# Attention, soft mixture of experts and feed-forward layer in one kernel: scores and values taken head by head, the third scores ahead of the first values, and another order of memory and loads

## The chip, the cores and the metric

The kernel runs on one core of a Trainium2 chip. The metric is the device time of one execution in microseconds: 371.45 us is the median of three runs (371.12 to 372.02). The engines are named as in the profile: PE is TensorE's matmul, PEld its weight load, DVE is VectorE, ACT is ScalarE, POOL is GpSimd, SP is SyncE, whose queue issues all DMA transfers here.

## The reference

Three layers follow one another. The attention has 4 batches, 8 heads, 576 tokens and head size 64, with a causal window of 64 tokens. Its result, 2304 rows of 512, goes through a soft mixture of 8 experts with 4 slots each, and that through a feed-forward layer of width 2048.

```python
scores = scale * np.matmul(q, k.transpose(0, 1, 3, 2))
mask = (rel >= 0) & (rel < window)               # rel = row - column, window = 64
scores = np.where(mask, scores, -1000000000.0)
attn = np.exp(scores - scores.max(-1)) ; attn /= attn.sum(-1) + 1e-09
x = np.matmul(attn, v)                           # then laid out as [2304, 512]

logits = x @ phi                                 # phi: 512 x 32 slots
d = softmax of logits over the rows ;  c = softmax of logits over the slots
slot_input = d.T @ x                             # 32 slots x 512
h = np.maximum(slot_input[e] @ w1[e], 0.0)       # per expert e, 4 slots each
slot_out[e] = h @ w2[e]
x = c @ slot_out

h = x @ w_in
g = h * (1.0 / (1.0 + np.exp(-1.702 * h)))
out = g @ w_out
```

## The kernel before

All transfers are issued by SP in the order of the program. Each engine's instructions stand in the order in which the code is written; no scheduler reorders them. There are four stages.

**Attention, rounds 0 to 17** (the loop `for i in range(ns)`). A unit is a pair of heads of one batch: 16 units, and two rounds for the last 64 tokens. The window makes each block of 64 queries see 128 keys. Round i has the scores of unit i (`emit_s`), the transposes of the exponentials of unit i-1 (`emit_t`), the transposes of x of unit i-2 (`xt_step`), and the values of unit i-1 (`emit_pv`); ACT has the exponentials (`emit_e`, one half for each head) and the copies of the transposes, VectorE the row maxima (`nm`) and the division (`emit_norm`). In `emit_s` the mask is put in first, by four bf16 matmuls of 64x64 tiles (L315), then come 16 score matmuls on the same four tiles (L330; each leaves two records). The tile is given by the head h (rows 0-63 or 64-127 of the array) and the half j of the queries (columns):

```python
for c in range(4):
    for h in range(2):
        for j in range(2):
            ... nc.tensor.matmul(st[h][rows[j], c, :], q, k, ..., tile_position=(64 * h, 64 * j))
```

The values (L365) have the same order of loops. They read the transposed exponentials of head 0 from `ab[0]` (named pa) and those of head 1 from `ab[1]` (pl), which ACT copies one behind the other (L351). In round 1 three matmuls on the identity (L608) fill a hole.

Beside it the routing of each batch runs in the same rounds (logits, L449; exponentials; slot sums, L499), and blocks of w_in and w_out, which come as 64-bit numbers, are narrowed in pieces on ACT, POOL and VectorE (`convert`, six blocks: four of w_in, two of w_out; `N_WO` = 2).

**The tail and w1.** Behind the last round the last batch's routing is finished; the combine weights of batches 0 to 2 are turned by `c_tile` (L419: 16 matmuls of 32 columns, 32 records each). Then the w1 stage (L763): four groups of 16 matmuls.

**w2** (L804): 16 blocks of 1 MB. The first seven lie in `arena`, the memory of the attention, at multiples of 2048 words (`dslot`), and each can be fetched once the attention's pieces there are no longer read; the other nine take the slots of w1, four after each group of w1 (`load_w`, `plan`). The order is that of SP's queue: what waits there holds all behind it.

**The feed-forward stage**, 48 steps of 36 matmuls at full width: L964 and L996. The w_out blocks that were not narrowed before are fetched behind w2 and narrowed in the first steps (`out_a`, `out_b`, `out_w`, `out_c`).

Tensors of the profile: s, t, v, m are the banks of PSUM, arena and rawt hold the attention's inputs, w the weights.

Of the kernel before, what the change touches and what calls it, by code (L numbers as in the profile page):

```python
# [32 lines left out]
W_AT = {i: 1 for i in range(2, 16)}  # L33
W_AT.update({16: 1, 17: 2})
L_AT = 12


CONV_AT = {2 + 2 * n: n for n in range(6)}
# [3 lines left out]
N_WO = 2  # L42
NT = B * S
TM = 4
# [8 lines left out]
QK0 = 0  # L53
MASK0 = QK0 + 2048
IDB0 = MASK0 + 512
X0 = IDB0 + 64
V0 = X0 + 2048
XT0 = V0 + 2 * 904
X1 = XT0 + KD * MT
XL0 = X1 + 2048  # L60
LTT0 = XL0 + 1024
XLT0 = LTT0 + 256
LT0 = XLT0 + 1024
D0 = LT0 + 128
DT0 = D0 + TM * NS
PHI0 = DT0 + 2 * NS
VL0 = PHI0 + 512
QL0 = XL0 + 512
ARENA = 7 * 2048
N_E = 16  # L70
LS0 = NE * 260

# [3 lines left out]
def attention_softmoe_ffn(  # L76
# [146 lines left out]
    lt = mem(LT0, 128)  # L223
# [34 lines left out]
    load_qk(0)  # L258
    load_v(0)
    load_qk(1)  # L260
# [44 lines left out]
    def emit_s(i):  # L305
        u, t = work[i]
        st = [bank("m" if i == 1 and h else "s", (128, 4, 128)) for h in range(2)]
        rows = [slice(64 * h, 64 * h + 64) for h in range(2)]
        for h in range(2):
            for j in range(2):  # L310
                o = st[h][rows[j]]
                m = mask[rows[h], j]
                if t is not None:
                    m = mask[rows[h], 0, 1:2].to_broadcast([64, 4, 128])
                nc.tensor.matmul(  # L315
                    o, identb[rows[h], rows[h]], m,
                    start=True, stop=False, tile_position=(64 * h, 64 * j))
        for c in range(4):
            for h in range(2):
                for j in range(2):  # L320
                    r = rows[h]
                    if t is None:
                        b = qbuf(u)[r]
                        q = b[:, 64 * (2 * c + j):64 * (2 * c + j) + 64]
                        o = c - 1 if c and not j else c
                        k = two(b, 512 + 64 * c, 768 + 64 * o)
                    else:
                        b = qbuf(NU + 2 * t + j)[r, 192 * c:192 * c + 192]
                        q, k = b[:, 0:64], b[:, 64:192]
# [23 lines left out]
    def emit_pv(i):  # L353
        u, t = work[i]
        pvt[i] = [bank("v", (128, 4, 65)) for _ in range(2)]
        for c in range(4):
            for h in range(2):
# [59 lines left out]
    def c_tile(p, l):  # L417
        for j in range(4):
            nc.tensor.matmul(  # L419
                p[32 * j:32 * j + 32], l, ident, start=True, stop=True, tile_position=(0, 32 * j))  # L420

# [15 lines left out]
    def routing(b):  # L437
# [33 lines left out]

        d = mem(D0, TM * NS).rearrange("p (t s) -> p t s", t=TM)

# [73 lines left out]
        def side(t0, a, tag):  # L547
            n = min(TM, nt - t0)

            def c_turn():  # L550
                st[t0] = pq = bank(tag)[:, 0:128 * n]
                for t in range(n):
                    p = pq[:, 128 * t:128 * t + 128]
                    if b < B - 1:
                        c_tile(p, l[:, t0 + t, :])
                    else:
                        nc.tensor.transpose(
                            p, st["c", t0][:, t].rearrange("p j s -> p (j s)"), ident)
# [3 lines left out]

            return [c_turn, lambda: c_high(a, st[t0]), lambda: c_low(a, st[t0])]
# [22 lines left out]
    load_qk(2)  # L586
    nc.sync.dma_start(out=phis, in_=phi.rearrange("p (k s) -> p k s", k=KD))
    raws = [wslot() for _ in range(3)]
    ns = len(work)
    def convert(i, first):  # L590
# [13 lines left out]
    for i in range(ns):  # L604
        emit_s(i)
        if i == 1:
            for _ in range(3):
                nc.tensor.matmul(bank("v")[:, 0:128], ident, ident, start=True, stop=True)  # L608
# [8 lines left out]
        for f in early.get(i, ()):  # L617
            f()
        if i:
# [14 lines left out]
        if 0 < i < NU - 1:  # L634
# [6 lines left out]
        elif i >= NU:  # L641
            for n in range(2):
                set_ones(NU + 2 * (i - NU) + n)
        if i == L_AT:
# [6 lines left out]
        if i < 3:  # L651
            for n in range(2 * i, 2 * i + 2):
                early_load(n)
        convert(i, False)
        load_w(W_AT.get(i, 0))
# [3 lines left out]
    load_w(1)  # L659
    emit_t(ns - 1)  # L660
    xt_step(ns - 2)()
# [8 lines left out]
    load_w(2)  # L670
# [18 lines left out]

    tail_logits(0)  # L690
# [7 lines left out]
    tail_logits(1)  # L698
    m = sp.tile([128, 1], F32, tag="mrun", name="mrun")
# [10 lines left out]
    dt = mem(DT0, 2 * NS).rearrange("p (t s) -> p t s", t=2)  # L710
# [11 lines left out]
    load_w(2)  # L722
# [60 lines left out]
    for f in sides[1][2:] + sides[2][2:] + norm:  # L783
        f()
# [196 lines left out]
    def emit_o(n, between):  # L981
# [28 lines left out]
        for t in range(nt):  # L1010
# [15 lines left out]
            for q in between.pop(t, ()):  # L1026
# [3 lines left out]
    ahead = {10: [lambda: out_w(0)], 11: [lambda: out_c(0), lambda: out_w(1)],  # L1030
             12: [lambda: out_c(1)]}
# [25 lines left out]
    out_a(2)  # L1057
# [3 lines left out]
    out_b(2)  # L1061
# [9 lines left out]
    out_w(2)  # L1071
    out_c(2)
    out_a(3)
    out_b(3, (0, 1))
# [4 lines left out]
    for p, (at, bt, ms) in enumerate((  # L1079
# [8 lines left out]
    for n in range(len(steps)):  # L1088
# [7 lines left out]
        if n in todo:  # L1096
            out_b(todo[n])
        between = {}
# [11 lines left out]
        emit_o(n, between)  # L1110
        if n == 0:
            out_b(3, (2, 3))
        if n in todo or n == 1:
            low = todo.get(n, 3)
            out_w(low)
# [62 lines left out]
```

## Time and profile before

| | |
|---|---|
| median of three runs | 371.45 us |
| the profiled execution: its time | 372.59 us |
| its span, first to last instruction | 370.6 us |
| granted TensorE clock over the span | 1.00 (2.4 GHz) |
| TensorE busy | 355.0 us |
| attention, round 2's scores to the last logits | 13 to 91 us |
| w1 starts | 107.24 us |
| last w2 matmul done | 140.94 us |

A row of the timeline has the start in us from the span's start, the length in us, the engine, the line, the operation, what is written and read, the shapes, and how many instructions were merged (x32); in brackets, if there is any, the idle time of the engine before it and what ended it. Matmuls are pipelined: the starts are measured, the lengths modelled, so the work is read from start to start. PE counts the matmul records; an fp32 matmul leaves two, a transpose one.

### The profile page before, as it was taken

What the parts mean: (1) busy time and instruction counts of PE and PEld (TensorE: products, weight loads), DVE (VectorE), ACT (ScalarE), POOL (GpSimd) and SP (SyncE); (2) the same over time, 40 slices, a digit from 0 to 9 for tenths busy, and PEclk for the clock granted to TensorE, in tenths of its full rate; (3) what the DMA queues carried; (4) which work ended last, traced back from release to release, by engine and by line L of the source; (5) the groups of instructions that cost most, each with busy time, mean ns of one, the idle gap of its engine ahead of it and who ended that gap; (6) DMA issues with size and microseconds to landing.
All of it is one profiled execution on the core that took longest, in us unless ns stands there. A gap on an engine that the chain in (4) does not pass through costs nothing.

```text
span 370.6 us, 7867 instructions
## 1 busy us (share of the span) xinstructions
PE 355.0 (96%) x3091; PEld 271.5 (73%) x3091; DVE 237.8 (64%) x518; ACT 195.6 (53%) x498; POOL 47.4 (13%) x92
## 2 busy tenths in 40 slices
PE   6999999999789998999999999999999999999995
PEld 5887777768543325888778887788887888888884
DVE  3566788877356404949485969697968786262624
ACT  3798878879223205765666644555545453333330
POOL 4545666441100000000000000000000000000000
PEclk9999999999999999999999999999999999999999
DMA  7999999999999995314031314131300000031404
GB/s 268 334 404 408 412 413 409 406 381 375 398 385 370 424 392 218 107 57 135 38 113 58 113 57 130 42 113 59 113 0 2 0 0 2 0 136 37 165 6 170
DMA packets 18804, 70.87 MB, mean 191 GB/s; under 512 B 2000, under 2 KB 3408, under 8 KB 14800
## 3 DMA queue, kind: packets, MB, share of 16 engines
q1 hardware_dynamic: 18768, 70.38, 50.1%
q8 instruction: 24, 0.39, 0.4%
q14 instruction: 12, 0.10, 0.1%
HBM read 65.65 MB, written 4.72 MB: 190 GB/s over the span
## 4 chain that ended last, share of the span: by engine, by line
PE 75%; DMA 9%; ACT 8%; DVE 4%; issue 2%; SPq 0%; POOL 0%; DVEq 0%; ACTq 0%; POOLq 0%
PE s L996 18%; PE t L996 17%; PE v L996 17%; DMA w<-in_w_dram 8%; PE m L964 5%; PE v L365 3%; ACT pa L342 3%; PE s L330 3%; PE m L350 2%; DMA arena<-in_qk_dram 2%; ACT pl L351 2%; ACT pa L351 1%; PE m L499 1%; PE m L449 1%; PE s L763 1%
## 5 line engine op out<-in xcount | busy, mean ns | idle before, releaser
L952 ACT ACTIVATE r<-m 128x384 fp32r<-128x384 f32 (+1 forms) x97 | 47.5, 493 | 85.0 <-PE m L964 84.9
L977 DVE TENSOR_TENSOR r<-g,r 128x384 fp32r<-128x384 f32 x96 | 51.4, 554 | 51.3 <-ACT g L952 43.0
L996 PE MATMUL t<-w,r 128*128 128x512 f32 x288 | 75.8, 395 | 0.0
L996 PE MATMUL s<-w,r 128*128 128x512 f32 x288 | 74.3, 392 | 0.0
L996 PE MATMUL v<-w,r 128*128 128x512 f32 (+1 forms) x291 | 73.4, 387 | 0.0
L996 PEld LDWEIGHTS t<-w,r 128*128 128x128 f32 x288 | 53.8, 188 | 14.7 <-issue 4.0
L996 PEld LDWEIGHTS v<-w,r 128*128 128x128 f32 x291 | 54.3, 188 | 11.4
L996 PEld LDWEIGHTS s<-w,r 128*128 128x128 f32 x288 | 52.6, 188 | 8.5
L952 ACT ACTIVATE g<-m 128x384 f32<-128x384 f32 x96 | 47.9, 501 | 0.0
L342 ACT ACTIVATE pa<-s,nm 128x128 f32<-128x128 f32 x140 | 40.7, 399 | 6.2 <-DVE nm L335 5.7
L964 PE MATMUL m<-cT,w 128*128 128x384 f32 (+2 forms) x113 | 25.7, 319 | 0.0
L335 DVE TENSOR_REDUCE nm<-s 128x4 f32<-128x512 f32 x35 | 22.5, 684 | 4.3 <-PE s L330 3.0
L964 PEld LDWEIGHTS m<-cT,w 128*128 128x128 f32 x113 | 20.8, 188 | 4.7 <-DVE w L901 0.6
L350 PE MATMUL m<-ident,pa 128*128 128x128 f32 x144 | 19.6, 279 | 0.0
L351 ACT COPY pa<-m 128x512 f32<-128x512 f32 x18 | 10.5, 586 | 13.7 <-PE m L350 13.6
L350 PEld LDWEIGHTS m<-ident,pa 128*128 128x128 f32 x144 | 15.5, 141 | 3.0 <-issue 2.4
L330 PE MATMUL s<-arena 64*64 64x128 f32 x352 | 13.7, 271 | 2.2 <-POOL rawt L247 1.6
L763 PE MATMUL s<-w,phis 128*32 128x512 f32 x128 | 14.6, 595 | 0.5 <-DVE phis L744 0.5
L384 DVE TENSOR_TENSOR arena<-v,rs 128x256 f32<-128x256 f32 x36 | 13.6, 420 | 0.6
L330 PEld LDWEIGHTS s<-arena 64*64 64x64 f32 x352 | 11.4, 133 | 3.5 <-POOL rawt L247 2.0
L365 PE MATMUL v<-arena,pa 128*64 128x65 f32 x184 | 13.2, 227 | 0.3 <-issue 0.3
L1016 DVE TENSOR_TENSOR w<-s,w 128x512 f32<-128x512 f32 x18 | 11.6, 684 | 2.8 <-PE s L996 2.8
(206 smaller groups left out, 472.7 us busy)
## 6 DMA issues: line engine op xcount, KB each, us to landing
w<-in_w_dram SPq DMA_DIRECT2D x24, 1024.0 KB, 10.4
w<-in_w_out_dram SPq DMA_DIRECT2D x16, 512.0 KB, 3.4
arena<-in_w_dram SPq DMA_DIRECT2D x7, 1024.0 KB, 8.5
iraw<-in_w_in_dram SPq DMA_DIRECT2D x12, 512.0 KB, 3.3
arena<-in_qk_dram SPq DMA_DIRECT2D x10, 512.0 KB, 8.7
out_dram<-w SPq DMA_DIRECT2D x16, 256.0 KB, 2.1
arena<-in_vt_dram SPq DMA_DIRECT2D x13, 258.5 KB, 7.5
rawt<-in_qk_dram SPq DMA_DIRECT2D x6, 512.0 KB, 9.9
```

Source lines behind the costliest of these rows:

```text
L330: nc.tensor.matmul(st[h][rows[j], c, :], q, k, start=False, stop=(c == 3), tile_position=(64 * h, 64 * j))
L335: nc.vector.tensor_reduce(out=nm[:, h], in_=st[h], axis=AX.X, op=ALU.max, negate=True)
L342: nc.scalar.activation(out=pb[h][:, c, :], in_=st[h][:, c, :], func=ACTF.Exp, bias=nm[:, h, c:c + 1], scale=1.0)
L350: nc.tensor.transpose(tt[:, c, :], pb[h][:, c, :], ident)
L351: nc.scalar.copy(ab[h], tt)
L365: nc.tensor.matmul(pvt[i][h][64 * j:64 * j + 64, c, :], ab[h][:, c, 64 * j:64 * j + 64], v, start=True, stop=True, tile_position=(0, 64 * j))
L384: nc.vector.tensor_tensor(out=o, in0=pv[h][:, :, 1 - h:65 - h], in1=rs[:, h].unsqueeze(2).to_broadcast([128, 4, 64]), op=ALU.mult)
L763: nc.tensor.matmul(ph[32 * j:32 * j + 32, :], siT[:, kk, :], w1t[4 * r + j][:, kk, :], start=(kk == 0), stop=(kk == KD - 1), tile_position ...
L952: nc.scalar.activation(out=(gh, g)[part][:, a:e], in_=ph[:, a:e], func=ACTF.Gelu_apprx_sigmoid)
L964: nc.tensor.matmul(ph[:, c - a:e - a], mst[:, f * 128:f * 128 + 128], cT(c, e - c), start=True, stop=True)
L977: nc.vector.tensor_tensor(out=gl, in0=g, in1=gh.bitcast(F32), op=ALU.subtract)
L996: nc.tensor.matmul(accs[t][:, h], a[:, c], b[:, h], start=(first and k == 0), stop=(last and k == 2 and h.stop == 512))
```

## The change

1. In `emit_s` and `emit_pv` the loop over heads becomes the outer one: head 0's masks and eight score matmuls, then head 1's; head 0's eight value matmuls, then head 1's.
2. Round 2's scores stand in round 1, ahead of the first values; their scaling is done on VectorE. The second block of q and k is fetched ahead of the first of v; the three filling matmuls go.
3. The combine weights of batches 0 to 2 are widened four times by a copy on VectorE (`c_wide`, into rawt) and turned by whole transposes, as those of batch 3 were.
4. The arena is laid out anew, so that its seven blocks come free in another order; small pieces (D0, LT0, DT0) move to rawt. The w1 and w2 loads are issued at other rounds.
5. Raw blocks of w_in are issued earlier, two at the start, and only one block of w_out comes that early (`N_WO` = 1); the second is fetched behind w2 and narrowed in the last stage's first steps, where the third and fourth follow a step later.

```diff
-W_AT = {i: 1 for i in range(2, 16)}
-W_AT.update({16: 1, 17: 2})
+W_AT = {**{i: 1 for i in range(2, 17)}, 10:0, 15:2, 16: 2, 17: 3}
+LATE = 99
-CONV_AT = {2 + 2 * n: n for n in range(6)}
+CONV_AT = {i: n for n, i in enumerate((3, 5, 7, 9, 11))}
-N_WO = 2
+N_WO = 1
...
+X0, QK0, XT0, V0, X1, XLT0, XL0 = [2048 * n for n in range(7)]
...
+D0, LT0, DT0 = LS0 - 152, LS0 + 288, LS0 + 416
...
     load_qk(0)
+    load_qk(1)
     load_v(0)
-    load_qk(1)
+    load_qk(2)
     load_v(1)
...
                 nc.tensor.matmul(
                     o, identb[rows[h], rows[h]], m,
                     start=True, stop=False, tile_position=(64 * h, 64 * j))
-        for c in range(4):
-            for h in range(2):
+            for c in range(4):
                 for j in range(2):
...
     def emit_pv(i):
...
-        for c in range(4):
-            for h in range(2):
+        for h in range(2):
+            for c in range(4):
                 for j in range(2):
...
             def c_turn():
                 st[t0] = pq = bank(tag)[:, 0:128 * n]
                 for t in range(n):
-                    p = pq[:, 128 * t:128 * t + 128]
-                    if b < B - 1:
-                        c_tile(p, l[:, t0 + t, :])
-                    else:
-                        nc.tensor.transpose(
-                            p, st["c", t0][:, t].rearrange("p j s -> p (j s)"), ident)
+                    nc.tensor.transpose(
+                        pq[:, 128 * t:128 * t + 128],
+                        st["c", t0][:, t].rearrange("p j s -> p (j s)"), ident)
...
+            def c_wide():
+                c = rawt[:, 512 * b:512 * b + 512].rearrange(
+                    "p (t j s) -> p t j s", t=TM, j=4)
+                nc.vector.tensor_copy(c, l.unsqueeze(2).to_broadcast([128, TM, 4, NS]))
+                st["c", 0] = c
...
-    load_qk(2)
...
+    for n in range(2):
+        early_load(n)
...
     for i in range(ns):
-        emit_s(i)
-        if i == 1:
-            for _ in range(3):
-                nc.tensor.matmul(bank("v")[:, 0:128], ident, ident, start=True, stop=True)
+        if i != 2:
+            emit_s(i)
         if i:
             emit_t(i - 1)
...
+        if i == 1:
+            scale_q(2, nc.vector)
+            emit_s(2)
         if i:
             emit_pv(i - 1)
...
-        if i < 3:
-            for n in range(2 * i, 2 * i + 2):
+        if i < 2:
+            for n in range(2 * i + 2, min(2 * i + 4, FP + N_WO)):
                 early_load(n)
...
-    out_a(2)
+    out_a(1)
...
-    out_w(2)
-    out_c(2)
-    out_a(3)
-    out_b(3, (0, 1))
+    out_w(1)
+    out_c(1)
+    out_a(2)
+    out_b(2, (0, 1))
...
-            ((2, 4, 5, 6), (8, 9, 10, 12), (8, 9)),
+            ((3, 4, 5, 6), (8, 9, 10, 12), (8, 9)),
...
+        if n == 1:
+            out_b(3, (0, 1))
...
+        if n < 2:
+            out_b(n + 2, (2, 3))
+        if n in todo or n < 2:
+            low = todo.get(n, n + 2)
+            out_w(low)
         if n == 0:
-            out_b(3, (2, 3))
...
+            out_a(3)
```

The order on TensorE in round 3, from the last of its mask matmuls to the first values, before (s is the bank of the scores, pa and pl are the heads' transposed exponentials):

```order
L315 LDWEIGHTS arena
L315 MATMUL s<-arena 64x512
L330 MATMUL s<-rawt 64x128 x16
L350 MATMUL m<-ident,pa 128x128 x8
L403 MATMUL m<-ident,arena 128x128 x4
L365 MATMUL v<-arena,pa 64x65 x2
L365 MATMUL v<-arena,pl 64x65 x2
```

The same round on TensorE after, from the last mask of head 0 on (L308 are the masks, L322 the scores, L357 the values):

```order
L308 MATMUL s<-arena 64x512
L322 MATMUL s<-rawt 64x128 x8
L308 LDWEIGHTS arena
L308 MATMUL s<-arena 64x512
L308 LDWEIGHTS arena
L308 MATMUL s<-arena 64x512
L322 MATMUL s<-rawt 64x128 x8
L342 MATMUL m<-ident,pa 128x128 x8
L395 MATMUL m<-ident,arena 128x128 x4
L357 MATMUL v<-arena,pa 64x65 x8
L357 MATMUL v<-arena,pl 64x65 x8
```

The sixteen scores in one piece became twice eight with head 1's masks between them, and the values, which went from head to head in pairs, became eight and eight.

TensorE behind the last round, before (L449 are logits, L419 the turn of batch 0's combine weights, lg):

```order
L449 MATMUL m<-arena,phis 32x128 x16
L350 MATMUL m<-ident,pa 128x128 x8
L403 MATMUL m<-ident,arena 128x128 x4
L419 MATMUL s<-ident,lg_84 32x128 x16
L365 MATMUL v<-arena,pa 64x65
```

and after, where rawt holds the widened weights and L540 turns them:

```order
L436 MATMUL m<-arena,phis 32x128 x16
L342 MATMUL m<-ident,pa 128x128 x8
L395 MATMUL m<-ident,arena 128x128 x4
L540 MATMUL s<-ident,rawt 128x128 x4
L357 MATMUL v<-arena,pa 64x65
```

Sixteen matmuls of 32 columns became four transposes; they stand at the same place, ahead of the last values.

The first transfers in SP's queue before (qk and vt are the units' inputs, w takes the raw blocks of w_in):

```order
L229 DMA rawt<-in_qk_dram 128x1024
L243 DMA rawt<-in_vt_dram 128x517
L229 DMA arena<-in_qk_dram 128x1024
L243 DMA arena<-in_vt_dram 128x517
L229 DMA arena<-in_qk_dram 128x1024
L587 DMA phis<-in_phi_dram 128x128
L229 DMA rawt<-in_qk_dram 128x1024
L243 DMA arena<-in_vt_dram 128x517
L154 DMA w<-in_w_in_dram 128x1024 x2
```

and after:

```order
L221 DMA rawt<-in_qk_dram 128x1024
L221 DMA arena<-in_qk_dram 128x1024
L235 DMA rawt<-in_vt_dram 128x517
L221 DMA arena<-in_qk_dram 128x1024
L235 DMA arena<-in_vt_dram 128x517
L578 DMA phis<-in_phi_dram 128x128
L146 DMA w<-in_w_in_dram 128x1024 x2
L221 DMA rawt<-in_qk_dram 128x1024
L235 DMA arena<-in_vt_dram 128x517
```

The second qk went ahead of the first vt, and the first two raw blocks ahead of the fourth qk.

## Rows read from the trace of the kernel before

**Rows 1.** The page: busy shares, and GB/s in 40 slices of 9.27 us.

```profile
PE 355.0 (96%) x3091; PEld 271.5 (73%) x3091; DVE 237.8 (64%) x518; ACT 195.6 (53%) x498; POOL 47.4 (13%) x92
...
GB/s 268 334 404 408 412 413 409 406 381 375 398 385 370 424 392 218 107 57 135 38 113 58 113 57 130 42 113 59 113 0 2 0 0 2 0 136 37 165 6 170
```

**Rows 2.** Windows: length, busy PE, PEld, DVE, ACT, POOL; clock, DMA, GB/s.

```profile
13.00:91.00 78.00, 74.65 (x1437) 59.46 (x1434) 60.22 (x172) 64.45 (x198) 38.34 (x66) 1.00 1.01 395
107.00:141.00 34.00, 32.48 (x290) 10.57 (x290) 11.47 (x25) 6.12 (x11) 0.00 (x0) 1.00 1.00 395
```

**Rows 3.** Timeline of TensorE, a plain round: start, length, line, tiles, records.

```profile
21.19 0.48 PE L315 MATMUL s<-arena 64*64 64x512 bf16 x4
21.43 1.11 PE L330 MATMUL s<-arena 64*64 64x128 f32 x32
22.47 1.09 PE L350 MATMUL m<-ident,pa 128*128 128x128 f32 x8
23.40 0.60 PE L403 MATMUL m<-ident,arena 128*128 128x128 f32 x4
23.93 0.34 PE L365 MATMUL v<-rawt,pa 128*64 128x65 f32 x4
24.34 0.34 PE L365 MATMUL v<-rawt,pl 128*64 128x65 f32 x4
...
25.31 0.47 PE L315 MATMUL s<-arena 64*64 64x512 bf16 x4
```

**Rows 4.** Timeline of TensorE's weight loads, same round; idle before in brackets.

```profile
22.47 0.85 PEld L350 LDWEIGHTS m<-ident,pa 128*128 128x128 f32 x8 [0.17 <-issue]
```

**Rows 5.** Timeline of ACT, the same round.

```profile
23.22 0.59 ACT L351 COPY pa<-m 128x512 f32<-128x512 f32 x1 [0.49 <-PE m L350]
23.70 0.59 ACT L351 COPY pl<-m 128x512 f32<-128x512 f32 x1
```

**Rows 6.** Timeline of TensorE, values that wait for nothing, and the next masks.

```profile
39.60 0.34 PE L365 MATMUL v<-rawt,pa 128*64 128x65 f32 x4
...
40.68 0.41 PE L315 MATMUL s<-arena 64*64 64x512 bf16 x4
```

**Rows 7.** Waits: who for whom, us in total, times, longest.

```profile
PEld v L365 <- ACT pl L351: 3.0, 14, 0.2
```

**Rows 8.** Timeline of TensorE, start-up.

```profile
8.38 0.33 PE L330 MATMUL s<-arena 64*64 64x128 f32 x2 [1.61 <-POOL rawt L247]
...
9.41 1.03 PE L608 MATMUL v<-ident 128*128 128x128 f32 x6
10.28 1.04 PE L350 MATMUL m<-ident,pa 128*128 128x128 f32 x8
...
14.23 0.44 PE L350 MATMUL m<-ident,pa 128*128 128x128 f32 x2
```

**Rows 9.** Timeline of TensorE, behind the last round.

```profile
92.80 0.63 PE L419 MATMUL s<-ident,lg 128*32 128x128 f32 x12
94.72 0.85 PE L419 MATMUL s<-ident,lg 128*32 128x128 f32 x20 [1.30 <-issue]
...
107.24 1.07 PE L763 MATMUL s<-w,phis 128*32 128x512 f32 x8 [0.47 <-DVE phis L744]
```

**Rows 10.** Groups by form: a copy that widens; busy, mean ns, idle before.

```profile
L631 DVE COPY arena<-phis 128x512 f32<-128x512 f32 x1 | 0.4, 418 | 0.0
```

**Rows 11.** Timeline of TensorE, the w2 stage and its end.

```profile
126.88 4.50 PE L804 MATMUL v<-arena,rawt 128*32 128x512 f32 x40
131.19 7.35 PE L804 MATMUL v<-w,rawt 128*32 128x512 f32 x64
...
140.94 0.71 PE L755 MATMUL s<-ident 128*128 128x128 f32 x4
```

**Rows 12.** Timeline of SP's queue, the last ten issues of w2.

```profile
110.86 12.76 SPq L149 DMA_DIRECT2D w<-in_w_dram  x10
```

**Rows 13.** Window of the last stage's second step, columns as in rows 2.

```profile
151.00:155.50 4.50, 4.50 (x21) 3.79 (x22) 4.40 (x9) 2.80 (x6) 0.00 (x0) 1.00 0.37 115
```

More of the change, by code (lines that the diff above doesn't have):

```diff
@@ L50 @@
 GREATEST = float(np.uint32(0x47EFFFFF).view(np.float32))
[L53 to L60, printed above, removed]
-LTT0 = XL0 + 1024
[L62 to L68, printed above, removed]
+X0, QK0, XT0, V0, X1, XLT0, XL0 = [2048 * n for n in range(7)]
+IDB0 = V0 + 2 * 904
+PHI0 = XLT0 + KD * 256
+MASK0 = PHI0 + KD * 128
+QL0 = XL0 + 512
+LTT0 = XL0 + 1024
+VL0 = LTT0 + 256
 ARENA = 7 * 2048
@@ L222, in attention_softmoe_ffn @@
     xlT = mem(XLT0, KD * 256).rearrange("p (k n) -> p k n", k=KD)
-    lt = mem(LT0, 128)
+    lt = rawt[:, LT0:LT0 + 128]
     ltt = mem(LTT0, 256)
@@ L415, in xt_step @@
         return evac
[L417 to L420, printed above, removed]
     def c_high(a, p):
@@ L470, in dexp @@
             st["s"] = s
-        d = mem(D0, TM * NS).rearrange("p (t s) -> p t s", t=TM)
+        d = rawt[:, D0:D0 + TM * NS].rearrange("p (t s) -> p t s", t=TM)
         def turn(*ks):
@@ L561, in c_turn @@
                         [128, 128 * n], F32R, tag="ct" if t0 else "pl", name="cT")
+            def c_wide():
[3 more added lines that the diff above has]
+                st["c", 0] = c
+            if b < B - 1:
+                return [c_turn, lambda: c_high(a, st[t0]), lambda: c_low(a, st[t0]), c_wide]
             return [c_turn, lambda: c_high(a, st[t0]), lambda: c_low(a, st[t0])]
@@ L633, in attention_softmoe_ffn @@
                 phis.unsqueeze(2).to_broadcast([128, KD, 4, NS]))
-        if 0 < i < NU - 1:
+        if 1 < i < NU - 1:
             scale_q(i + 1, nc.gpsimd)
@@ L643, in attention_softmoe_ffn @@
                 set_ones(NU + 2 * (i - NU) + n)
+        if LATE <= i < ns - 1:
+            load_w(W_AT.get(i, 0))
         if i == L_AT:
@@ L650, in attention_softmoe_ffn @@
             load_v(i + 2 + (i + 2 >= NU))
-        if i < 3:
-            for n in range(2 * i, 2 * i + 2):
+        if i < 2:
+            for n in range(2 * i + 2, min(2 * i + 4, FP + N_WO)):
                 early_load(n)
         convert(i, False)
-        load_w(W_AT.get(i, 0))
+        if i < LATE or i == ns - 1:
+            load_w(W_AT.get(i, 0))
     rings.update(s=[0, 1], t=[2, 7], v=rings["v"])
     cts[0] = s1.tile([128, 1536], F32R, tag="pa", name="cT")
-    load_w(1)
+    sides[0][3]()
     emit_t(ns - 1)
+    sides[1][3]()
     xt_step(ns - 2)()
@@ L669, in attention_softmoe_ffn @@
     total()
-    load_w(2)
+    load_w(1)
     sides[0][1]()
@@ L688, in tail_logits @@
         nc.vector.tensor_reduce(out=mm[:, t:t + 1], in_=lpt[:, c], axis=AX.X, op=ALU.max)
+    sides[2][3]()
     tail_logits(0)
@@ L698, in attention_softmoe_ffn @@
     tail_logits(1)
+    load_w(1)
     m = sp.tile([128, 1], F32, tag="mrun", name="mrun")
@@ L709, in attention_softmoe_ffn @@
     gather()
-    dt = mem(DT0, 2 * NS).rearrange("p (t s) -> p t s", t=2)
+    dt = rawt[:, DT0:DT0 + 2 * NS].rearrange("p (t s) -> p t s", t=2)
     pd = bank("m", (128, 2, NS))
@@ L721, in attention_softmoe_ffn @@
                 start=True, stop=True, tile_position=(0, 32 * g))
-    load_w(2)
+    load_w(1)
     sr = sp.tile([128, 1], F32, tag="srun", name="srun")
@@ L782, in attention_softmoe_ffn @@
     turn(1)
-    for f in sides[1][2:] + sides[2][2:] + norm:
+    for f in sides[1][2:3] + sides[2][2:3] + norm:
         f()
@@ L1027, in emit_o @@
                 q()
-    ahead = {10: [lambda: out_w(0)], 11: [lambda: out_c(0), lambda: out_w(1)],
-             12: [lambda: out_c(1)]}
+    ahead = {10: [lambda: out_w(0)], 11: [lambda: out_c(0)]}
     wb = bank("s")
@@ L1060, in attention_softmoe_ffn @@
     m0[1]()
-    out_b(2)
+    out_b(1)
     emit_m1(1, "v")
@@ L1110, in attention_softmoe_ffn @@
         emit_o(n, between)
+        if n < 2:
[3 more added lines that the diff above has]
+            out_w(low)
         if n == 0:
-            out_b(3, (2, 3))
-        if n in todo or n == 1:
-            low = todo.get(n, 3)
-            out_w(low)
+            out_a(3)
         if n + 1 in more:
```

## The prediction, made before the changed kernel was run

> **What bounds the kernel now.** I read the page's busy shares and bandwidth by slice first, then the chain of waits, then TensorE's timeline of one round of the attention, and last the stretches behind it. TensorE is busy for 355.0 of 370.6 us, and from slice 2 to slice 15 the DMA engines move 334 to 424 GB/s, so two resources are full for the first 140 us [rows 1]. The reader is to see which of them a shorter or longer piece of work would move, stage by stage.
>
> In the attention, 13 to 91 us, TensorE is busy 74.65 of 78 us, at the granted clock 1.00 (2.4 GHz), and the DMA carries 395 GB/s [rows 2]. One round without routing runs from the mask matmuls at 21.19 to the next ones at 25.31: 4.12 us [rows 3]. In it the matmuls stand end to end: masks, scores, transposes of the round before, transposes of x, values. The row of the values shows the only hole: head 0's first pair starts at 23.93, head 1's at 24.34, since ACT copies head 0's transposes (pa) at 23.22 and head 1's (pl) only at 23.70 for 0.59 us [rows 3, 5]. So TensorE sets a round's length, and the wait for pl is inside it.
>
> Behind the attention the w1 stage starts at 107.24 [rows 9] and needs nothing of the DMA. The w2 stage does: five blocks pass in 126.88 to 131.19, 0.86 us each, so the 14 blocks from 126.88 on would be through at 138.95; they are through at 140.94, which is 2.0 us of waiting for the last blocks to land [rows 11]. From there to the end of the span (229.7 us) TensorE is full again. Both limits meet at 141 us: whatever TensorE gains before it is capped by the DMA unless that gains too, but whatever TensorE loses counts, less 2.0 us.
>
> **The change part by part.**
>
> Scores head by head. The 16 score matmuls of a round are 64x64 tiles; each leaves two records of 128 columns. Today the order is block, head, half, so that consecutive matmuls lie on four different tiles: 32 records between 21.43 and 22.47, less the 0.17 in which the engine goes over to the transposes (its weight load stands idle so long [rows 4]), 0.87 us or 27 ns each, which is 108 ns on each of four tiles [rows 3]. The values are two tiles wide: 32 records of 65 columns between 39.60 and 40.68, less as much again, 0.91 or 28 ns each, 57 ns on each of two tiles [rows 6]. That is 1.19 and 1.14 columns per ns and tile: a tile has its own pace, whether two or four are at work. With head 0's eight matmuls ahead of head 1's, only two tiles are at work at a time if TensorE keeps its order: 32/2 x 108 ns = 1.73 us, 0.86 more than now. The masks, four at once in 0.24 us (21.19 to 21.43), become two and two: some 0.2 more, of which 0.1 lies beside the last scores of head 0. Sum: +0.95 us a round. Nothing else in a round is idle that could take it up.
>
> The trace of before has no place where a matmul for a free tile stands behind one for a busy tile, so the cost has two ends: 0, if TensorE lets head 1 pass, and 1.1, if the second masks hide nothing. A gain is excluded, since no engine waits for the first head's scores alone: ACT comes to its exponentials only behind the pl copy. The nearest row is the values': head 0's second pair has its operand since 23.8 and still starts only behind head 1's first pair, which waited until 24.34 [rows 3, 5]. TensorE does not pass a matmul that is held. I take 0.95.
>
> The Trainium skill (TensorE: Matmul & The Clock Gate, Part 3: Packing small matmuls — row/col tiling) says that matmuls start and end in program order, and only weight loads are pulled ahead. By that the two heads cannot overlap, and the sum is the one below; were matmuls pulled ahead as weight loads are, the first rival would hold. The values' row agrees with the rule for a matmul that waits for a semaphore; for one that waits for a tile no row shows it.
>
> Values head by head. All of head 0's values then run before pl is needed. Values with the wait take 25.31 - 23.93 = 1.38 us up to the next masks, those without 40.68 - 39.60 = 1.08 [rows 3, 6]; the wait occurs 14 times [rows 7], the first at the start-up's values. So 13 x 0.30 = -3.9 us. Head 0's half takes about 0.47, to 24.4, and pl is there at 24.29. Ends: -3.9, and 0 if ACT's copy comes later.
>
> Third scores ahead of the first values. Today the second scores start at 8.38 after a wait for POOL's scaling of the second block, then come three filling matmuls (9.41 to 10.28) and the transposes; the next transposes start at 14.23 [rows 8]. Afterwards the second block is fetched one transfer earlier (258.5 KB, about 0.8 us at the 334 GB/s of slice 2 [rows 1]): scores from 7.6, 1.95 us long, no filling matmuls, transposes at 9.7, third scores (0.2 + 2.0), first values (0.2 + 0.93), next transposes at about 14.2. I count 0, between -1.0 and +1.0, and from here on the extra applies to the scores of rounds 3 to 17: 15 x 0.95 = +14.25 us.
>
> The turn of the combine weights. The first three row blocks are no longer turned by 32 small-tile records each, but widened on VectorE and transposed whole. Block 0's turn stands on the path: 92.80 to 95.57 with a stall of 1.30 in the middle [rows 9]. Four whole transposes cost 4 x 0.116 (eight took 22.47 to 23.40 [rows 3]) = 0.46, but wait for VectorE, which first has the maximum of the last logits; the widening is one copy of 128x512, 0.42 [rows 10]. I take -0.9; the ends are -1.7 (the stall goes too) and +0.2. The turns of blocks 1 and 2 lie in holes of the tail that VectorE and ACT set; 0.
>
> Arena, order of loads, w_out. w_out's second block (0.52 MB, 1.3 us at 400 GB/s) goes behind w2, the raw blocks come earlier, and the arena's regions come free in the order in which w2 takes them. All of it helps the DMA, which then is not the limit: w1 starts 9.4 us later, so the nine w2 blocks that go into w1's slots are issued from 110.9 + 9.4 = 120.3 on [rows 12], 9.44 MB at 395 GB/s end at 144.2, and TensorE wants the last at 138.95 + 9.4 = 148.4. So the 2.0 us of waiting go, and the rest of the DMA's gain buys nothing. Cover of the converted block: its VectorE work (about 1.5 us) moves into the second step of the last stage, where VectorE was busy 4.40 of 4.50 us [rows 13]; its products come a step ahead of their use, so 0, at most +0.6.
>
> Sum: +14.25 - 3.9 - 0.9 - 2.0 = +7.45 us, on the profiled execution: span 370.6 to 378.05, its time 372.59 to 380.0. The runs shown have their median at 371.45, 1.14 below that execution, so 371.45 + 7.45 = **378.9 us**.
>
> **The rivals.**
>
> 1. The two heads overlap all the same, since TensorE queues ahead and tiles are independent. For it: four tiles do run side by side. Against it: the held pair in the values. Then TensorE comes to w1 3.9 + 0.9 = 4.8 earlier, and the DMA is the limit: its last w2 block lands 1.3 earlier for w_out, and up to 0.9 earlier for the slow first two slices (268 and 334 GB/s [rows 1]). 371.45 - 1.7 = 369.8, faster. It decides as soon as a round's scores take under 1.2 us.
>
> 2. They overlap in part, say half: 15 x 0.45 = 6.75, less 3.9, 0.9 and 2.0, is 0: 371.4, the same.
>
> 3. The wait for pl stays: ACT was busy 64.45 of 78 us in the attention [rows 2], and if its copies come as late after the transposes as head 0's values are short, nothing of the 3.9 is saved: 382.8. Against it: pl was there 0.1 before it would be needed, and longer rounds give ACT time.
>
> That the change leaves TensorE's order as it was is excluded by the order above.
>
> **How the numbers follow.** Forecast 0.65, rival 1 0.20, rival 2 0.07, rival 3 0.08. A measurement of this kernel tells 0.3%, 1.1 us, from no change. Slower 0.65 + 0.08 = 0.73; the same 0.07; faster 0.20. The likeliest case alone: with 0.86 to 1.05 a round (+-1.4), the start-up (+-1.0) and the tail (+1.1, -0.8) 375.8 to 382. For 8 in 10 the range goes up to 383, which takes in rival 3, and down to 369.6, which takes in rival 2 and half of rival 1.
>
> **What would show it.** Right: the scores' 32 records with the second masks take 2.0 us up to the transposes, in two bursts; a plain round lasts 4.75 to 4.8; no wait of the values for pl; w1 starts at 116 to 117; no wait of the w2 matmuls for the DMA; the last stage still 229 to 230 us; granted clock 1.00 throughout. Wrong: scores still near 1.0 us, w1 before 104 and the w2 stage ended by a transfer (rival 1); or pl waits still 13 times (rival 3); or the last stage longer by over 1 us, which nothing here foresees.

## The result, and the profile after

The changed kernel takes 374.68 us (median of 20 runs, 372.33 to 379.12), the kernel before 370.99 beside it (20 runs); the ratio is 1.0085, 95% interval 1.006 to 1.0109: slower by about 3.2 us, where +7.45 was forecast. Two of the changed kernel's 20 runs, over 1.5% above its fastest, are left out of the ratio; of those that are left its profiled execution is one of the faster, while before's was one of the slower, so the profiles say where time went and the ratios how much. The profiled execution took 373.05 us with a span of 371.1, only 0.5 more than before's: this pair of profiles holds 0.5 of the 3.2 us. Below, 1% is 3.7 us.

The page of the changed kernel, to be held against [rows 1]; PEclk is the granted clock in tenths:

```profile
PE 359.3 (97%) x3001; PEld 278.6 (75%) x3001; DVE 241.5 (65%) x523; ACT 195.2 (53%) x498; POOL 44.9 (12%) x90
...
PEclk9999999999989999999999999999999999999999
...
GB/s 275 410 412 409 390 380 239 397 345 386 422 425 349 427 391 273 109 115 123 48 113 58 113 58 123 48 111 61 113 2 0 0 0 2 0 133 39 163 9 170
```

TensorE is 4.3 us busier, the second slice moves 410 GB/s for 334, and one slice (102 to 111 us) has a lower clock. The windows of [rows 2] now, in the same columns:

```profile
13.00:91.00 78.00, 76.87 (x1370) 64.87 (x1370) 56.69 (x162) 61.59 (x189) 37.31 (x67) 1.00 0.97 371
107.00:141.00 34.00, 33.52 (x295) 11.48 (x294) 11.07 (x24) 5.60 (x10) 0.00 (x0) 0.95 0.98 395
```

In the attention TensorE is busy for 98.6% of the time, the DMA carries less than before. TensorE's timeline of a plain round, the counterpart of [rows 3]:

```profile
20.40 0.40 PE L308 MATMUL s<-arena 64*64 64x512 bf16 x2
20.64 0.71 PE L322 MATMUL s<-arena 64*64 64x128 f32 x10
21.09 0.40 PE L308 MATMUL s<-arena 64*64 64x512 bf16 x2
21.18 1.18 PE L322 MATMUL s<-arena 64*64 64x128 f32 x22
22.30 1.09 PE L342 MATMUL m<-ident,pa 128*128 128x128 f32 x8
23.22 0.60 PE L395 MATMUL m<-ident,arena 128*128 128x128 f32 x4
23.75 0.69 PE L357 MATMUL v<-rawt,pa 128*64 128x65 f32 x16
24.27 0.64 PE L357 MATMUL v<-rawt,pl 128*64 128x65 f32 x16
24.84 0.40 PE L308 MATMUL s<-arena 64*64 64x512 bf16 x2
```

Head 0's half of the scores is 16 records, but head 1's masks start at 21.09 behind only ten of them; the other six stand behind the masks. So head 1 passes six records, three on each of two tiles (a pair, below, is one record on each of a head's two tiles). From the first mask to the transposes it is 1.90 us for 1.28, +0.62 and not +0.95. The values stand without a hole (0.93 us from first to last start, no wait for pl). The round is 4.44 us for 4.12, where 4.77 was forecast. Rounds 3 to 17 together, from the third round's masks to the last logits, are 75.15 us (15.96 to 91.11) for 73.00 (17.07 to 90.07): +2.15 and not 15 x 0.62, since most rounds of before were longer than their matmuls need (values to values, six of the nine rounds without routing took 4.12 to 4.63 us, three 3.75).

Behind the rounds, against [rows 9]:

```profile
94.35 0.66 PE L540 MATMUL s<-ident,rawt 128*128 128x128 f32 x4 [0.40 <-DVE rawt L550]
...
100.99 0.60 PE L540 MATMUL t<-ident,rawt 128*128 128x128 f32 x4
102.38 0.31 PE L714 MATMUL m<-ident,arena 32*128 32x32 f32 x2 [0.78 <-ACT arena L706]
...
103.81 0.63 PE L540 MATMUL v<-ident,rawt 128*128 128x128 f32 x4
106.53 1.05 PE L743 MATMUL m<-i4s,acc 128*128 128x32 f32 x8 [2.08 <-DVE acc L741]
108.05 5.01 PE L764 MATMUL s<-w,phis 128*32 128x512 f32 x32 [0.48 <-DVE phis L745]
```

The stall of 1.30 is gone (not by the turn, as a_ctile shows) and the turn's matmuls are short, but TensorE now waits: 0.40 for VectorE's widening copy, 0.78 for ACT, and 2.08 for VectorE ahead of psi. VectorE's and GpSimd's timelines say why:

```profile
104.44 1.93 DVE L734 TENSOR_SCALAR i4s<-i,rsl 128x32 f32<-128x32 f32 x1
104.60 2.24 DVE L741 TENSOR_TENSOR acc<-m,acc 64x256 f32<-64x256 f32 x2
```

```profile
104.51 1.83 POOL L749 MEMSET rawt<- 128x2080 f32 x1 [11.95 <-PE v L540]
```

i4s, 32 columns, takes 1.93 us and ends as GpSimd's clearing of ht does. The clearing has to wait for the last turn, which now reads its widened block out of the same tile, so it falls on i4s. The windows of TensorE (length, busy, granted clock, DMA, GB/s) show what followed the waits:

```profile
102.00:107.40 5.40, 2.63 (x24) 1.00 1.02 428
107.50:110.80 3.30, 2.82 (x17) 0.50 1.02 425
111.00:125.00 14.00, 14.00 (x127) 1.00 0.93 377
```

TensorE was busy for 2.63 of 5.40 us, and then its granted clock was 0.50 (1.2 GHz): the first w1 group took 5.01 us. w1 starts 0.8 us later than before and w2 2.2 later (126.62 for 124.44), yet w2 now waits for no transfer; its end, against [rows 11]:

```profile
133.38 7.91 PE L805 MATMUL v<-w,rawt 128*32 128x512 f32 x80
141.22 0.71 PE L756 MATMUL s<-ident 128*128 128x128 f32 x4
```

From 141.22 on to the end of the span it is 229.9 us, for 229.7.

### The profile page after: what moved, and what is told of

It is laid out like the page before. It is cut to its first block, busy times and chain, and to the rows that moved or that the text cites. A ratio compares the mean times of both kernels' runs of the same rounds, so it can differ in the third digit from the quotient of the medians.

```text
span 371.1 us, 7689 instructions
## 1 busy us (share of the span) xinstructions
PE 359.3 (97%) x3001; PEld 278.6 (75%) x3001; DVE 241.5 (65%) x523; ACT 195.2 (53%) x498; POOL 44.9 (12%) x90
## 4 chain that ended last, share of the span: by engine, by line
PE 89%; DVE 5%; ACT 3%; issue 1%; DMA 1%; DVEq 0%; ACTq 0%
PE s L997 18%; PE t L997 17%; PE v L997 17%; PE s L322 6%; PE m L965 5%; PE s L764 4%; PE v L357 4%; PE v L805 4%; PE m L342 4%; PE s L308 2%; PE m L395 2%; ACT pa L334 2%; PE m L486 1%; DMA rawt<-in_qk_dram 1%; DVE nm L327 1%
## 5 line engine op out<-in xcount | busy, mean ns | idle before, releaser
L322 PE MATMUL s<-arena 64*64 64x128 f32 x352 | 20.1, 269 | 0.1
L322 PEld LDWEIGHTS s<-arena 64*64 64x64 f32 x352 | 18.6, 133 | 1.2 <-DVE arena L231 0.4
L764 PE MATMUL s<-w,phis 128*32 128x512 f32 x128 | 15.9, 642 | 0.5 <-DVE phis L745 0.5
L933 ACT CAST w<-wf 128x512 fp32r<-128x512 f32 x15 | 9.3, 623 | 9.2 <-DVE wf L171 9.2
L308 PE MATMUL s<-arena 64*64 64x512 bf16 x70 | 14.1, 400 | 0.1
```

The lines of the kernel that those rows point to most:

```text
L308: nc.tensor.matmul(o, identb[rows[h], rows[h]], m, start=True, stop=False, tile_position=(64 * h, 64 * j))
L322: nc.tensor.matmul(st[h][rows[j], c, :], q, k, start=False, stop=(c == 3), tile_position=(64 * h, 64 * j))
L764: nc.tensor.matmul(ph[32 * j:32 * j + 32, :], siT[:, kk, :], w1t[4 * r + j][:, kk, :], start=(kk == 0), stop=(kk == KD - 1), tile_position ...
```

## The experiments

All ratios are to the kernel before run beside each, with 95% intervals. The theories: A, the loss is the collision of MEMSET and i4s with the low clock behind it; B, it is the longer scores; C, it is the low clock behind the rounds; D is on how far a matmul may pass a held one.

| kernel | scores | values | turn | other | ratio (interval) | median us |
|---|---|---|---|---|---|---|
| changed | by head | by head | widened | | 1.0085 (1.006-1.0109) | 374.68 |
| a_memset | by head | by head | widened | MEMSET later | 1.0073 (1.0047-1.0099) | 373.34 |
| a_inter | interleaved | by head | widened | | 1.0002 (0.9981-1.0023) | 370.45 |
| a_both | interleaved | by head | widened | MEMSET later | 0.9964 (0.9942-0.9987) | 369.16 |
| b_heads | by head | by head | as before | rest as before | 1.0147 (1.0116-1.0179) | 375.36 |
| b_pv | interleaved | by head | as before | rest as before | 0.9989 (0.9971-1.0007) | 370.3 |
| a_ctile | by head | by head | as before | | 1.0059 (1.0028-1.0089) | 373.05 |
| a_best | interleaved | by head | as before | | 0.9929 (0.9907-0.995) | 367.78 |
| a_rest | interleaved | interleaved | as before | | 0.9957 (0.9934-0.9979) | 368.45 |
| a_warm | by head | by head | widened | 39 idle matmuls | 1.015 (1.0106-1.0193) | 376.91 |
| a_fill | by head | by head | widened | 18 idle matmuls | 1.0062 (1.0033-1.0091) | 373.2 |
| a_both_warm | interleaved | by head | widened | MEMSET later, 27 | 0.9964 (0.9939-0.9988) | 369.53 |

**a_inter: scores interleaved again.**

```
-            for c in range(4):
+        for c in range(4):
+            for h in range(2):
                 for j in range(2):
```

> The changed kernel with the scores of the two heads interleaved again (both heads' masks first), values still head by head. Theory B (longer score rounds): a plain round falls from 4.44 to about 3.82 us (4.12 less 0.30), the last logits start 0.6 x 15 = 9 us earlier if TensorE's issue stalls stay away (tied to what the DMA queues move), some 4.5 us earlier if they come back (tied to the order of the scores); median 370 to 366, with the collision at i4s still there. Theory A (the loss is behind the rounds): the rounds are shorter but the end is set by w2's weights or the collision; median 373 to 375.

Measured: 0.83% or 3.1 us under the changed kernel, so the scores are the greater part of the loss. But the last logits come only 4 us earlier (87.15 for 91.11), not 9. Some rounds fell to 3.75 us, plain ones stayed at 4.13, and TensorE waited 2.3 us for ACT ahead of the logits: theory B with a smaller size.

**b_heads: only the two loops turned, in the kernel before.**

```
-        for c in range(4):
-            for h in range(2):
+            for c in range(4):
                 for j in range(2):
...
-        for c in range(4):
-            for h in range(2):
+        for h in range(2):
+            for c in range(4):
                 for j in range(2):
```

> The kernel before with only the two loops turned: scores and values head by head; loads, arena and order of the rounds as before. Theory B: a plain round 4.12 + 0.61 - 0.30 = 4.43 us, the last logits 0.31 x 15 = 4.7 us later, less up to 4.4 if the issue stalls go with the order of the scores; median 371.5 to 375.7, no stretch at 0.50. Theory A: no collision here, i4s stays at 0.24 us and the end follows the rounds by little: 371 to 372.

Measured: +1.47%, 5.4 us, in the range of theory B. In its trace the last logits start 6.2 us later than before's (96.28 for 90.07) and the w2 stage, which no longer waits for a transfer, ends 2.7 later (143.61 for 140.94). The rest of the change, then, gains: 0.6% between this and the changed kernel.

**b_pv: only the values turned (the second half of that diff), in the kernel before.**

> The kernel before with only the values head by head. By the prediction's step (13 waits of 0.30 us for pl go, nothing is late next): -3.9 us, ratio 0.9895. If ScalarE is next (TensorE then waits for its x copy ahead of the logits, and head 1's mask for its last exponentials, as the kernel with interleaved scores showed): 1 to 2 us, ratio 0.995 to 0.997.

Measured: -0.4 us, less than either expectation, and its interval holds zero. Its timelines show where the wait went, TensorE first, then ACT:

```profile
20.22 0.69 PE L365 MATMUL v<-arena,pa 128*64 128x65 f32 x16
20.73 0.64 PE L365 MATMUL v<-arena,pl 128*64 128x65 f32 x16
21.30 0.78 PE L315 MATMUL s<-arena 64*64 64x512 bf16 x4
21.78 1.17 PE L330 MATMUL s<-arena 64*64 64x128 f32 x32
22.88 1.09 PE L350 MATMUL m<-ident,pa 128*128 128x128 f32 x8
...
24.34 0.75 PE L365 MATMUL v<-rawt,pa 128*64 128x65 f32 x15
```

```profile
20.47 1.16 ACT L342 ACTIVATE pa<-s,nm 128x128 f32<-128x128 f32 x4
21.48 0.62 ACT L407 COPY arena<-m 128x512 f32<-128x512 f32 x1
21.94 1.20 ACT L342 ACTIVATE pa<-s,nm 128x128 f32<-128x128 f32 x4
23.63 0.59 ACT L351 COPY pa<-m 128x512 f32<-128x512 f32 x1 [0.49 <-PE m L350]
24.11 0.59 ACT L351 COPY pl<-m 128x512 f32<-128x512 f32 x1
24.59 1.16 ACT L342 ACTIVATE pa<-s,nm 128x128 f32<-128x128 f32 x4
```

The values stand end to end, as forecast, but from the masks to the transposes it is now 1.58 us for 1.28 of [rows 3]. The scores go round three banks, two a round, so head 1's pair of masks writes the bank of head 0 of the round before, which ACT's exponentials of that head still read; these begin at 20.47 behind the pl copy and end at 21.63, and the pair is held until 21.68. The round stays 4.12 us (20.22 to 24.34, values to values). So such a round of 4.12 us was a loop through two engines: exponentials of head 0 on ACT, head 1's masks and the scores of the next round on TensorE, the transposes behind them, ACT's copies pa and pl, exponentials of head 0 again. The wait for pl was slack inside it, and taking it away moved 0.30 us to the mask.

**a_mask1: both heads' masks first, scores by head.** (One run, 374.0 us.)

```
+        for h in range(2):
             for c in range(4):
                 for j in range(2):
```

The added loop makes the scores' one its own, behind the four masks.

> The changed kernel with both heads' masks ahead of both heads' scores, which stay head by head. Theory D (a matmul on a free half passes a few queued ones of a busy half, three pairs here): from the first mask to the transposes about 1.65 us in a plain round (masks 0.24, five pairs of head 0, three pairs of both together, five of head 1), against 1.89 in the changed kernel. A queue that passes nothing: 2.15 or more. One that passes freely: 1.28 as with interleaved heads.

Measured, TensorE in a round whose masks wait for nothing:

```profile
16.23 0.41 PE L308 MATMUL s<-arena 64*64 64x512 bf16 x4
16.47 1.54 PE L323 MATMUL s<-rawt 64*64 64x128 f32 x32
17.94 0.33 PE L343 MATMUL m<-ident,pa 128*128 128x128 f32 x1
```

1.71 us for 1.65 expected, far from 2.15 and from 1.28, as theory D said; it is one run, and the sizes were taken from the changed kernel. In plain rounds, where head 1's masks wait for ACT, it is 2.00 and the round 4.54, longer than the changed kernel's 4.44. Head 1's masks behind head 0's scores hide that wait, which is why the longer scores cost a plain round only 0.32.

**a_memset: the clearing held back behind siT.**

```
+    nc.gpsimd.tensor_tensor(
+        out=ht[:, 0:32], in0=siT[:, 0], in1=siT[:, 0], op=ALU.subtract)
     nc.gpsimd.memset(ht[:, 0:LS0], 0.0)
```

> The changed kernel, with GpSimd's clearing of ht (128x2080) held back by a 128x32 operation on GpSimd that reads siT, so that it starts behind VectorE's i4s and siT. Theory A (what the change loses is the collision of this MEMSET with VectorE's i4s, 1.93 us for 0.24, and the clock of 0.50 that follows TensorE's wait of 2.08): i4s back under 0.4 us, TensorE's wait ahead of psi under 0.6, no stretch at 0.50, w1 starts about 1.7 us earlier and its first group takes 3.6 for 5.0: median 3 us under the changed kernel's 374.7, about 371.6. Theory B (the loss is the longer score rounds, and DMA or something else sets w2's end): the wait goes, but w2 ends where it did; median 374 to 375.

Measured: in the profile all that theory A said (i4s 0.24 us, the wait 0.70, no stretch at 0.50, w1 at 106.94), in the time 0.12% less, within the intervals. In nine of the twelve executions the mean clock was 0.991 to 0.995, as in the changed kernel, so a low clock of that size came back in most of them, though no trace shows where. Theory A alone falls. With the scores interleaved (**a_both**, this edit and a_inter's) it gave 0.38%, 1.4 us: 369.16, near the 370 of its second case. Its profile has the low clock and no collision.

> The changed kernel with both edits: scores interleaved again and the MEMSET behind siT. Both theories added: 374.7 - 3.1 - (4.5 to 9) = 363 to 367 if nothing else ends last; if w2's weights (DMA) set the end of w2 as they did in part before (2.0 us of waits there), the gain stops at about 4 us: 370.

**a_warm: idle matmuls in the waits, too many** (one of five places shown).

```
     psi = bank("m", (128, KD, 32))
+    for _ in range(17):
+        nc.tensor.matmul(psi.rearrange("p k s -> p (k s)"), ident, ident, start=True, stop=True)
...
```

> The changed kernel with idle matmuls of ident (results overwritten) in five waits of TensorE behind the rounds: 2 ahead of each turn, 5 ahead of the last x transposes, 8 of 64 columns ahead of the dt transposes, 17 ahead of psi, 3 ahead of w1; the collision of MEMSET and i4s stays. Theory C (TensorE's waits there let its clock fall to 0.50, in most executions, and that is what is lost behind the rounds): no stretch at 0.50 from 94 to 145 us, the first w1 group 3.6 us for 5.0, median 1.4 to 2 us under the changed kernel, a ratio of 1.003 to 1.005. Theory B (the longer score rounds are all of it): the ratio stays at 1.0085.

Measured: a miss of mine. An fp32 matmul of 128 columns leaves two records and takes 0.22 us, not the 0.11 I had sized them by; seventeen fill 3.8 us of a wait of 2.08, and w1 began at 111.54, 3.5 us later than in the changed kernel. The clock held, i4s took 0.24 us, so the collision had gone too, and the time rose. **a_both_warm** (a_both and these, 5 ahead of psi) had the same fault in smaller measure: w1's first group took 3.64 us for 5.65 but began at 106.74 for 104.32, and the time is that of a_both.

> Interleaved scores, MEMSET behind siT, and the idle matmuls (5 ahead of psi here). Theory C: the stretch of 6.8 us at 0.50 from 101.6 on goes; the first w1 group 3.64 for 5.65 us and about 0.5 us ahead of it: 2 to 2.5 us under 369.2, that is 366.7 to 367.2, ratio 0.990. If w2's weights end last instead: 368 to 369, with waits on w in w2.

**a_fill: as a_warm, as many as fit (8 ahead of psi).**

> The changed kernel with idle matmuls of 0.22 us each that fit into TensorE's waits (1 ahead of each turn, 3 ahead of the last x transposes, 2 ahead of dt, 8 ahead of psi, 2 ahead of w1), so that they delay nothing; the collision of MEMSET and i4s stays. Theory C (the clock at 0.50 costs time behind the rounds): no such stretch, w1's first group 3.6 for 5.0 us, 1 to 1.6 us under the changed kernel, ratio 1.004 to 1.006. If w2's weights take the gain back: w1 and w2 start 1.4 us earlier and w2 ends where it did, ratio 1.008.

Measured: 0.23%, 0.85 us under the changed kernel, the size of theory C, with intervals that overlap. The clock was 1.00, w1's groups 3.64. But the collision did not stay: the later turn put MEMSET at 104.72, 0.1 us behind the end of i4s. VectorE's and GpSimd's rows:

```profile
104.38 0.24 DVE L741 TENSOR_SCALAR i4s<-i,rsl 128x32 f32<-128x32 f32 x1
104.54 0.87 DVE L751 TENSOR_TENSOR acc<-m,acc 64x256 f32<-64x256 f32 x2
104.72 1.83 POOL L759 MEMSET rawt<- 128x2080 f32 x1 [11.81 <-PE v L544]
```

So this run removes collision and low clock together and does not part them. acc, a TENSOR_TENSOR that reads PSUM, runs beside the clearing without loss; i4s, a TENSOR_SCALAR from SBUF to SBUF, did not. Whether the operation or the memory decides, no run shows.

**a_ctile: the turn as before.**

```
+                    if b < B - 1:
+                        for j in range(4):
+                            nc.tensor.matmul(
+                                pq[32 * j:32 * j + 32, 128 * t:128 * t + 128], l[:, t0 + t, :],
+                                ident, start=True, stop=True, tile_position=(0, 32 * j))
...
-                nc.vector.tensor_copy(c, l.unsqueeze(2).to_broadcast([128, TM, 4, NS]))
...
```

> The changed kernel with the turn of the weights done again as 32 matmuls of 32 columns each on the three blocks, without VectorE's widening copies. By the prediction's step (the turn is worth 0.9 us): 0.9 us slower than the changed kernel, ratio 1.011. Theory C (TensorE waits there anyway, and busy matmuls hold its clock): the chain behind the rounds ends no later, no stretch at 0.50: 1 to 2 us faster than the changed kernel, ratio 1.003 to 1.006.

Measured: 0.26%, 1.0 us faster than the changed kernel; the step of the prediction had it 0.9 slower. TensorE's rows:

```profile
100.89 1.08 PE L542 MATMUL t<-ident,lg 128*32 128x128 f32 x32
102.18 0.31 PE L719 MATMUL m<-ident,arena 32*128 32x32 f32 x2 [0.21 <-ACT arena L711]
...
104.95 1.05 PE L748 MATMUL m<-i4s,acc 128*128 128x32 f32 x8 [0.19 <-DVE acc L746]
106.48 3.64 PE L769 MATMUL s<-w,phis 128*32 128x512 f32 x32 [0.47 <-DVE phis L750]
```

The dt transposes come 0.2 us earlier than in the changed kernel with a turn 0.48 longer, so ACT's chain set them. MEMSET runs at 99.71, clear of i4s, and the mean clock was at least 0.998 in all twelve executions, for 0.986 to 0.995 in the changed kernel's twenty. Block 0's turn gains nothing on the path: from the last logits to the values behind the turn it is 3.78 us here (90.90 to 94.68) and 3.83 in the changed kernel (91.11 to 94.94). The stall of 1.30 is absent here with the old turn, as in a_best, b_heads and b_pv, whose values are head by head; in the traces it comes with interleaved values, before (1.30) and in a_rest (1.28).

**a_best: the edits of a_inter and a_ctile together; a_rest: these, and the values' two loops turned back.**

> The changed kernel with scores interleaved again and the turn done again as 32 matmuls on the three blocks (values head by head, arena, loads as changed). If the two losses add up as in the single runs (scores 0.83%, turn 0.26%): ratio 1.0085 - 0.0109 = 0.9976, 369.9. If the turn is worth more here, since without it the clock was 0.50 for 6.8 us (first w1 group 5.6 for 3.6 us, psi 1.9 for 1.05): 367.5 to 368.5, ratio 0.991 to 0.994. If w2's weights end last: no better than 0.9964 of the kernel with both other edits.

> As the kernel with interleaved scores and the turn of 32 matmuls, but values interleaved too: what is left of the change is the arena, the loads, the third scores ahead of the first values, and w_out's blocks. By the prediction's terms (start-up 0, w2's DMA waits -2.0): 369.0, ratio 0.995. If w2 only waits for its weights because TensorE comes early: ratio 0.999 to 1.001.

Measured: a_best 0.9929, 367.78 us, faster than both kernels: 2.6 us under before, 5.8 under the changed one. The turn was worth 0.73% here (a_inter to a_best), where the clock had been 0.50 from 101.6 to 108.2. That is the second case of its expectation. a_rest 0.9957, the first case: loads, arena, start-up and w_out's blocks alone gain 1.6 us, and the values by head another 1.0, within the noise. What limits a_best, in the waits of TensorE in the rounds (us, times, longest) and at w2's end:

```profile
PE m L437 <- ACT arena L400: 1.7, 3, 0.9
PE m L437 <- ACT pa L335: 0.5, 1, 0.5
PE v L358 <- issue: 0.5, 1, 0.5
```

```profile
134.89 0.64 PE L811 MATMUL v<-w,rawt 128*32 128x256 f32 x8 [0.85 <-DMA w<-in_w_dram]
135.46 0.71 PE L762 MATMUL s<-ident 128*128 128x128 f32 x4
```

ACT is next in the rounds, and at the end the last w2 block, with a wait of 0.85 us as in rival 1; but w2 is done at 135.46, 5.5 us earlier than before, where rival 1 allowed 1.7. The round that waits for nothing shows what the interleaved order can do, 1.22 us from mask to transposes:

```profile
38.77 0.41 PE L308 MATMUL s<-arena 64*64 64x512 bf16 x4
39.01 1.04 PE L323 MATMUL s<-arena 64*64 64x128 f32 x32
39.99 1.09 PE L343 MATMUL m<-ident,pa 128*128 128x128 f32 x8
```

## Why the prediction was wrong in size

The sign came out, the time did not: it lies inside the range, 4.2 us under the forecast. By a chain of runs from before to the changed kernel, in which each step but the last row is one edit, so that the sum comes out by itself:

| step | forecast us | measured us, from |
|---|---|---|
| scores by head | +14.25 | +4.8, a_best to a_ctile |
| values by head | -3.9 | -1.0, a_rest to a_best; -0.4, b_pv |
| turn | -0.9 | +1.0, a_ctile to changed |
| start-up, arena, loads, w2's waits | -2.0 | -1.6, before to a_rest |
| sum | +7.45 | +3.2 |

Each difference of two ratios is uncertain by some 0.35%, 1.3 us, so the values' and the turn's signs are not certain from these pairs alone; the turn's is from a_inter to a_best, whose intervals lie apart. The steps also depend on one another: scores by head cost 3.1 us with the widened turn (a_inter to changed), 4.8 with the old one, and 5.9 with the old loads (b_pv to b_heads). That the last row agrees is luck: the -2.0 were w2's waits, and a_rest still has one (0.81 us); its trace gains ahead of w2 (last logits at 88.10 for 90.07).

The step that failed is the first, "15 x 0.95 = +14.25 us", in both of its factors. The 0.95 rested on "only two tiles are at work at a time if TensorE keeps its order", for which I took the held pair in the values as the nearest row. That pair waited for a semaphore. In the two kernels with two tiles at a time, matmuls held by a busy tile stopped the others only beyond three pairs of records, so head 1 overlapped in part and a round without waits lost 0.69 (4.44 for 3.75) in place of 0.95. This was rival 2, at 0.07, and I had put it down as "say half" without a row. The Trainium skill (TensorE: Matmul & The Clock Gate, Part 3: Packing small matmuls — row/col tiling) has matmuls start and end in program order; the masks at 21.09, ahead of six score records written before them, do not agree, and the measurement decides.

The 15 rested on "Nothing else in a round is idle that could take it up". TensorE alone did not set most plain rounds: those of 4.12 us were set by the loop through ACT, and of before's nine rounds without routing between the second values (15.69) and the seventeenth (88.69) only three ran at TensorE's own 3.75. The same loop took the values' gain: the wait for pl, "inside it" as I wrote, was priced as time, and came back one to one at head 1's masks. Rival 3 had this mechanism in another place (pl itself). Both errors partly cancel, since longer scores hide ACT's wait. The measured +4.8 for the +14.25 is what they left.

The turn's sign was wrong. On the path the old turn without its stall takes 1.01 us up to the next values (93.67 to 94.68 in a_ctile), less than the 1.47 that [rows 9] leave beside the stall; the new one takes 0.59 (94.35 to 94.94), and the wait of 0.40 for the copy takes up the difference. The turns' matmuls lay beside chains of VectorE and ACT; a shorter turn gave longer waits, a wait for the widening copy, MEMSET on top of i4s, and the lower clock; how much of the loss each has, the runs do not part. I had named the holes ("0") but not what TensorE's idling and GpSimd's later start would do there.

Nor did "whatever TensorE gains before it is capped by the DMA" hold. b_pv, with the old loads, starts w1 at 106.14 (before 107.24) and ends w2 at 137.95 without a wait, 3.0 us earlier than before; w2's waits come and go between kernels in no order of w1's start, and why is open.

Right, or nearly: the start-up (third masks 1.1 us earlier, just past the bound of -1.0), w2 without waits in the changed kernel, the last stage unchanged at 229.9, VectorE's work for the converted block free. Open: TensorE's stalls of [rows 9]'s kind, put down to "issue" (2.3 us in the rounds of before, 0.8 in a_best, none in the changed kernel). They came in every kernel with interleaved scores and hardly with the other order; their cause was not tried. Open too: the spread of the changed kernel's executions. Of the 18 in the ratio, those with a mean clock of 0.994 or 0.995, like the profiled one with its 3.3 us at 0.50, have their median at 373.1 us, and those at 0.986 to 0.991 at 375.5; a_inter, at 0.990, has 6.6 us at 0.50 in its profile. The clock alone does not explain it (373.97 us at 0.990, 377.09 at 0.991), and none of the changed kernel's executions at 0.986 to 0.991 has a trace.

## What to carry to other kernels

Before pricing a wait on the busiest engine, follow the loop that it stands in round by round: if another engine's chain closes the loop, the wait only moves, and extra work on the busy engine is partly free. Work taken off an engine in a stretch where it waits anyway buys nothing, and can cost the clock of the dense stretch behind it. When an operand moves into a tile that another engine clears later, look at what that clearing will then run beside.

## What was not expected of the hardware

- TensorE started matmuls for free tiles ahead of six records (three pairs) that were held by busy tiles (21.09 above; 1.71 us in a_mask1).
- GpSimd's clearing held an SBUF-to-SBUF operation of VectorE for its whole length: 1.93 us, where it took 0.24 in before, a_memset, a_both, a_ctile, a_fill and a_best. acc, which reads PSUM, ran beside it at 0.87 us in a_fill. The Trainium skill (SBUF — State Buffer, SBUF: two separate sides) tells of a port pair that VectorE and GpSimd share, and that whichever starts first holds for its whole instruction. These rows agree with the hold of a whole instruction; by their recorded starts i4s (104.44) came ahead of the clearing (104.51) and was held all the same.
- In the changed kernel's tail 5.40 us with TensorE busy for 2.63 were followed by a granted clock of 0.50; 3.64 us of w1 then took 5.01, and up to 5.65 in a_both.
